# Retention outputs from a packed state, one join on another engine, and a reordered middle step

## The chip, the cores and the metric

The kernel runs on 1 core of one Trainium2 chip. The metric is the device time of one launch in microseconds. The kernel before has three timed runs: 305.37, 305.54 and 307.35 us, median 305.54 us.

## The reference, cut to what matters

```python
def _attn_ref(q, k, v):                      # q, k, v: (8, 8, 576, 64)
    scores = scale * np.matmul(q, k.transpose(0, 1, 3, 2))
    gamma = 1.0 - 2.0 ** (-5.0 - np.arange(H))
    rel = pos[:, None] - pos[None, :]
    Dmat = np.where(rel >= 0, gamma[:, None, None] ** rel, 0.0)
    return np.matmul(scores * Dmat, v)

def _moe_ref(x, w_in, w_out):                # (4608,512) (512,2048) (2048,512)
    h = x @ w_in
    g = h * np.clip(h + 3.0, 0.0, 6.0) / 6.0
    return g @ w_out

x = attn_out.transpose(0, 2, 1, 3).reshape(4608, 512)
out = _moe_ref(x, w_in, w_out)
```

So there is a retention (attention without softmax, with a decay for each head) over 8 batches, 8 heads, 576 positions and 64 columns a head, and behind it a feed-forward layer of two matrix products over the 4608 tokens.

## The kernel before, in words

**Pieces.** Each batch is cut into four pieces of 128 positions ("main", numbered i = 0 to 3 within the batch) and a rest of 64; the rests of two batches make one piece ("rest"). For each piece the output is the sum of an inner part (masked scores times v) and a part from the state of the pieces before it. The eight heads go as four pairs; a pair fills the 128 partitions, 64 for each head.

**The state.** `update_mm` (L362) makes each piece's own contribution k'v for all heads by 64-column matmuls into a PSUM tile `u`, in the bank with the tag `tu`, of which there is one. `update_state` (L379) has VectorE add the state before it (L390) and scale by the decay (L391); the result `ts` is packed: 128 partitions x 4 pairs x 64, with head 2p in partitions 0 to 63 and head 2p+1 in 64 to 127. ScalarE then copies its two halves (L403, L404) into a tile `tbd` of 128 x 4 x 128, in which the two heads of a pair stand on the diagonal and the rest is zero. `inter` (L325) multiplies `tbd` with the queries: one 128x128 matmul for each pair (L339). A piece with i = 0 has no state before it and `inter` issues nothing for it; so of four main pieces three have these matmuls. The first batch is made apart, by `state_early`, which writes block-diagonal tiles directly.

**Scores.** `scores` (L307) makes scores in 64-row matmuls, the two heads of a pair into two PSUM banks, and VectorE masks them (L318). `scores_second` (L656) does the same for a second piece in two banks of the tag `ph`. `intra` (L345) adds the inner part into the same bank as `inter`, and ScalarE copies the bank to `xt`, the input of the feed-forward (L356).

**Feed-forward.** It goes in blocks of 512 tokens. `gemm1` makes 16 units for each block: four matmuls into a `ph` bank (L417), a ScalarE and a VectorE instruction on it (L424, L425). For blocks 2 to 7 the second product is one Strassen-Winograd step with seven half-size products (`product`, L511) that accumulate in three banks `b`, `a` and `c`, and `gather` (L529) reads partial sums out: products 1, 6 and 7 from `b` and 5 from `c` by ScalarE copies (L535), the joins for the quarters of the output by VectorE (L538, L543), by GpSimd (L541, the quarter C22 from two SBUF copies) and by ScalarE (L546).

**Order.** The order on each engine is the order of the program text. `seven_block` (L708) mixes the products of one block with the pieces of the block after the next: up to one rest (`alone`) and the four main pieces c0 to c3, two at a time. Its middle step, between products 6 and 5, is: `inter` of c0 and c1, the second in a bank of the tag `ph`; scores and `update_mm` of c2 and c3; `intra` of c0 and c1. Its last step, between products 3 and 4, is `inter` and `intra` of c2 and c3. Five blocks (2 to 6) have four main pieces; block 7 has a rest alone. Block 1 uses `step` (L679), which does the same between units of an ordinary second product. The second batch (pieces 4 to 7) is made in `first_step` (L621), between units of block 0; there the `inter` matmuls are at L641. The tag `ph` has four banks, `o`, `tu` one each and `sc` two banks.

Of the kernel before, what the change touches and what calls it, by code (L numbers as in the profile page):

```python
# [11 lines left out]
FP16 = mybir.dt.float16  # L12
# [5 lines left out]
def kernel(  # L18
# [20 lines left out]
    P = 128  # L39
# [129 lines left out]
        nc.scalar.copy(gqv[:, 0], gq[:, :, None].to_broadcast([P, H, D]))  # L169

    tbd = []
    for i in range(5):
        t = const.tile([P, NPAIR, P], FP16, name=f"tbd{i}")
        if i >= EARLY:
            nc.vector.memset(t, 0.0)
        tbd.append(t)

    warmed = [0]

# [19 lines left out]

    st = {}  # L200
    later = []
    free_tbd = list(range(5))
    state_of = {}

    def run_later(n):
        for _ in range(n):
# [54 lines left out]
    def out_last(c):  # L261
        before, qk = st[c]["before"], st[c]["qk"]
        at, vs = st[c]["at"], st[c]["vs"]
        kb, g0 = place_of(c)
        halves = [psum.tile([P, NPAIR, P], FP32, tag="o", name=f"o_{c}"),
                  psum.tile([P, NPAIR, P], FP32, tag="ph", bufs=4, name=f"o2_{c}")]
        for i, o in enumerate(halves):
            for p in range(2):
                nc.tensor.matmul(o[:, p, :], tbd[before][:, 2 * i + p, :], qk[:, 0, 2 * i + p, :],
                                 start=(p == 0), stop=False, skip_group_check=True)  # L270
        for i, o in enumerate(halves):
            for p in range(2):
                for h2 in range(2):
                    r = slice(h2 * HALF, h2 * HALF + HALF)
                    nc.tensor.matmul(o[r, p, :], vs[:, 4 * i + 2 * p + h2, :],
                                     at[:, h2, 2 * i + p, :],
                                     start=False, stop=(p == 1), skip_group_check=True)
            nc.scalar.copy(xt_of(kb)[:, 2 * i:2 * i + 2, g0:g0 + P], o[:, 0:2, :])  # L278

    def state_early(c):  # L280

        kn, vs = loaded[c]["kn"], st[c]["vs"]
        u = psum.tile([P, NPAIR, P], FP32, tag="tu", name=f"u_{c}")
        old = st[c]["before"] = state_of.get(0)
        for p in range(NPAIR):
            nc.tensor.matmul(u[:, p, :], kn[:, 2 * p:2 * p + 2, :], vs[:, 2 * p:2 * p + 2, :],
                             start=(p == 0), stop=(old is None and p == NPAIR - 1),
                             skip_group_check=True)
        if old is not None:
            nc.tensor.matmul(u, ident16, tbd[old], start=False, stop=True,  # L290
                             skip_group_check=True)
            free_tbd.append(old)
        new = free_tbd.pop(0)
        state_of[0] = new
        later.append(lambda: nc.vector.tensor_tensor(out=tbd[new], in0=u, in1=gfull,
                                                     op=ALU.mult))

    def transpose_k(c):
# [26 lines left out]
    def inter(c, tag="o"):  # L325
        kind, b, i, _ = pieces[c]
        o = psum.tile([P, NPAIR, P], FP32, tag=tag, bufs=4 if tag == "ph" else 1, name=f"o_{c}")
        st[c]["o"] = o
        st[c]["first"] = True
        if kind == "main" and i == 0:  # L330
            return
        qk = st[c]["qk"]
        if kind == "main":
            states = [(st[c].get("before", state_of[b]), slice(0, P))]
        else:
            states = [(state_of[2 * b], slice(0, HALF)), (state_of[2 * b + 1], slice(HALF, P))]
        for j, (state, cols) in enumerate(states):
            for p in range(NPAIR):
                nc.tensor.matmul(o[:, p, cols], tbd[state][:, p, :], qk[:, 0, p, cols],  # L339
                                 start=(j == 0 and p == 0), stop=False, skip_group_check=True)  # L340
            if kind == "rest" or st[c].get("last_reader"):
                free_tbd.append(state)
        st[c]["first"] = False

    def intra(c, copy_later=False, more=False):  # L345
# [33 lines left out]
    def update_state(c, copies_later=False):  # L379
# [5 lines left out]
        ts = work.tile([P, NPAIR, D], FP16, tag="ts", bufs=2, name=f"ts_{c}")  # L385
        if i == 0:
            nc.vector.tensor_tensor(out=ts, in0=u, in1=scale, op=ALU.mult)  # L387
        else:
            ta = work.tile([P, NPAIR, D], FP32, tag="ta", bufs=2, name=f"ta_{c}")
            nc.vector.tensor_tensor(out=ta, in0=u, in1=st[c - 1]["ts"], op=ALU.add)  # L390
            nc.vector.tensor_tensor(out=ts, in0=ta, in1=scale, op=ALU.mult)  # L391
        st[c]["ts"] = ts
        old = state_of.get(b)
        new = free_tbd.pop(0)
        state_of[b] = new
        if old is not None and st[c].get("o") is not None:
            free_tbd.append(old)
        elif old is not None:
            st[c]["before"] = old
            st[c]["last_reader"] = True  # L400

        def copies():
            nc.scalar.copy(tbd[new][0:HALF, :, 0:D], ts[0:HALF])  # L403
            nc.scalar.copy(tbd[new][HALF:P, :, D:2 * D], ts[HALF:P])  # L404

        if copies_later == "given":
            return copies
        if copies_later:
            later.append(copies)
        else:  # L410
            copies()

    gts = {}

# [114 lines left out]
    def gather(kb, which):  # L529

        my = seven[kb]
        if which in (1, 6, 7, 5):
            my[which] = work.tile([P, 2, half_n], FP32, tag=f"part{which}", bufs=1,
                                  name=f"part{which}_{kb}")
            nc.scalar.copy(my[which], my["c" if which == 5 else "b"])  # L535
# [2 lines left out]
            nc.vector.tensor_tensor(out=my["lo"][:, :, lo_n], in0=my[1], in1=my["a"], op=ALU.add)  # L538
        if which == 7:
            my["hi"] = work.tile([P, 2, DM], FP32, tag="osb2", bufs=3, name=f"ohi_{kb}")  # L540
            nc.gpsimd.tensor_tensor(out=my["hi"][:, :, hi_n], in0=my[7], in1=my[5], op=ALU.add)  # L541
# [79 lines left out]
    def first_step(c):  # L621
# [3 lines left out]
        if old:  # L625
# [6 lines left out]
            update_state(c - 1, copies_later=True)  # L632
        if new:
            q_by_pe(c + 1)
        if old and new:
# [72 lines left out]
    def seven_block(kb, mine, next_):  # L708
# [4 lines left out]
        copies = {}  # L713

        def both(which):
            for tt in range(2):
                product(kb, which, tt)

        def state(c):
            copies[c] = update_state(c, copies_later="given")  # L720

        def begin(one, other):
            masks[one] = scores(one, given=True)
            masks[other] = scores_second(other, given=True)
            update_mm([one, other])

        def end(*cs):
            for c, tag in zip(cs, ("o", "ph")):
                inter(c, tag)

        def done(*cs):
            for c in cs:
                st.pop(c - 3, None)
                loaded.pop(c)

        masks = {}
# [6 lines left out]
        if c0 is not None and not alone:  # L743
            begin(c0, c1)
        both(1)
        gather(kb, 1)
        if alone:
            end(*alone)
            if c0 is not None:
                begin(c0, c1)  # L750
            intra(alone[0])
        if c0 is not None:
            masks[c0]()
            state(c0)
            copies[c0]()
            masks[c1]()
            load_until(c1 + NBUF)
        elif alone:
            load_until(alone[0] + NBUF)
        done(*alone)  # L760
        both(2)
        gather(kb, 2)
        if c0 is not None:
            state(c1)
        both(6)
        gather(kb, 6)
        if c0 is not None:
            end(c0, c1)
            begin(c2, c3)
            intra(c0)  # L770
            intra(c1)
            copies[c1]()
        sum_of(kb, 3, 0, 8)
        if c0 is not None:
            masks[c2]()
        sum_of(kb, 4, 0, 8)
        if c0 is not None:
            state(c2)
            done(c0, c1)
            load_until(c3 + NBUF)  # L780
        both(5)
        gather(kb, 5)
        if c0 is not None:
            masks[c3]()
        both(7)
        gather(kb, 7)
        if c0 is not None:
            copies[c2]()
            state(c3)
        both(3)  # L790
        if c0 is not None:
            end(c2, c3)
            intra(c2)
            intra(c3)
            done(c2, c3)
# [1 line left out]
            ahead(c)  # L797
        gather(kb, 3)
        both(4)
        if c0 is not None:  # L800
            copies[c3]()
        gather(kb, 4)
        for c in next_[2:]:
            ahead(c)
# [89 lines left out]
```

## Time and profile before

| | |
|---|---|
| median of the runs | 305.54 us |
| the profiled execution's own time | 305.33 us |
| its span, first to last instruction | 303.6 us |
| granted TensorE clock, mean | 0.994 |
| TensorE busy in the stretch 90 to 240 us | 28.8 to 29.1 us of every 30 |
| VectorE busy in the same stretch | 26.9 to 27.9 us of every 30 |
| ScalarE busy in the same stretch | 18.0 to 19.0 us of every 30 |
| `tbd` copies on ScalarE, L403 and L404 | 28 each, 11.3 and 11.2 us together |

The profiled execution took 1.7 us more than its span, for what lies before the first and behind the last instruction. In the rows of the profile a matmul stands as PE with the number of rows and columns of the array that it uses (128*128, 64*128, 128*64) and then the shape that goes through; PEld is the load of the weights. A duration of one matmul, such as 219 ns, runs from issue to the end in the array; matmuls are pipelined, so what a run of matmuls costs is read from the starts of successive rows.

### The profile page before, as it was taken

The numbers are of one execution on the slowest core, as the hardware profiler recorded it, in microseconds if no ns is written. First come the engines' busy times: TensorE is split into PE (matmuls) and PEld (weight loads), VectorE is DVE, ScalarE is ACT, GpSimd is POOL, SyncE is SP. The second block draws the span as 40 slices with busy tenths as digits, with TensorE's granted clock in tenths as the row PEclk, the third lists the DMA queues.
The fourth block names the chain that finished last, engine by engine and source line by source line (L and its number), as shares of the span: only waits on it lengthen the run. The fifth ranks groups of instructions, "written<-read, shape, count | busy, mean of one in ns | idle before, by whom it ended". The sixth has DMA issues, their size and how long they took to land.

```text
span 303.6 us, 6408 instructions
## 1 busy us (share of the span) xinstructions
PE 287.9 (95%) x2526; PEld 177.9 (59%) x2526; DVE 228.6 (75%) x372; ACT 178.0 (59%) x307; POOL 117.7 (39%) x141
## 2 busy tenths in 40 slices
PE   5989998999999989998999899989999899999995
PEld 2644445544544777467745784578448754884444
DVE  4748666797749998899889997999799849727700
ACT  5558436784558546855676557745773587327611
POOL 8983577736612295076500980485000100010000
PEclk9799999999999999999999999999999999999999
DMA  9999999999999499999992999799730030012022
GB/s 71 146 192 207 189 159 216 168 129 155 155 175 96 102 133 106 231 81 125 91 244 54 96 125 217 85 128 85 201 76 2 17 141 2 0 56 86 1 69 71
DMA packets 152976, 35.56 MB, mean 117 GB/s; under 512 B 143601, under 2 KB 148465, under 8 KB 152945
## 3 DMA queue, kind: packets, MB, share of 16 engines
q0 software_dynamic: 117264, 18.36, 85.0%
q1 hardware_dynamic: 35280, 16.26, 26.1%
q10 hardware_dynamic: 400, 0.52, 0.5%
q8 instruction: 20, 0.33, 0.4%
q14 instruction: 12, 0.09, 0.1%
HBM read 36.70 MB, written 9.44 MB: 152 GB/s over the span
## 4 chain that ended last, share of the span: by engine, by line
PE 76%; DMA 8%; DVE 5%; ACT 4%; POOL 4%; issue 1%; POOLq 0%; DVEq 0%; ACTq 0%
PE ph L417 35%; PE b L525 12%; PE pout L474 8%; PE c L525 7%; DMA wout<-in_moe_w_out_dram 5%; PE a L525 4%; DMA win<-in_moe_w_in_dram 3%; PE o L350 3%; POOL qv L102 2%; ACT xt L356 2%; DVE at L318 2%; PE u L374 2%; PE sc L314 1%; PE o L339 1%; POOL kn L102 1%; PE pout L559 1%
## 5 line engine op out<-in xcount | busy, mean ns | idle before, releaser
L425 DVE SCALAR_TENSOR_TENSOR gt<-u,ph 128x512 f16<-128x512 f32 x144 | 97.4, 686 | 31.6 <-ACT u L424 29.4
L424 ACT ACTIVATE u<-ph,cb 128x512 f32<-128x512 f32 x144 | 98.3, 687 | 25.7 <-PE ph L417 24.5
L417 PE MATMUL ph<-xt,win 128*128 128x512 f16 x496 | 108.4, 379 | 0.6 <-ACT xt L278 0.4
L417 PEld LDWEIGHTS <-win 128*128 128x128 f16 x560 | 54.8, 98 | 65.1 <-issue 0.7
L102 POOL DMA_DIRECT2D kn<-in_k_dram x40 | 34.6, 869 | 78.0 <-PE u L374 39.8
L525 PEld LDWEIGHTS <-s 128*128 128x128 f16 x384 | 37.5, 98 | 9.3 <-issue 4.6
L474 PE MATMUL pout<-wout,gt 128*128 128x512 f16 x176 | 39.6, 379 | 0.0
L102 POOL DMA_DIRECT2D qv<-in_v_dram x40 | 34.7, 874 | 4.2 <-DMA wout<-in_moe_w_out_dram 1.7
L102 POOL DMA_DIRECT2D qv<-in_q_dram x40 | 34.5, 866 | 4.8 <-DMA wout<-in_moe_w_out_dram 3.2
L541 POOL TENSOR_TENSOR ohi<-part,part 128x512 f32<-128x512 f32 x6 | 8.8, 1462 | 62.2 <-ACT part L535 60.7
L525 PEld LDWEIGHTS <-gt 128*128 128x128 f16 x288 | 26.9, 98 | 4.3
L474 PEld LDWEIGHTS <-gt 128*128 128x128 f16 x176 | 16.8, 98 | 19.1
L318 DVE TENSOR_TENSOR at<-sc,mask_wide 128x1024 f16<-128x1024 f32 x19 | 23.2, 1219 | 5.1 <-PE sc L314 5.0
L535 ACT COPY part<-b 128x512 f32<-128x512 f32 x18 | 10.6, 586 | 27.2 <-PE b L525 27.2
L356 ACT CAST xt<-o 128x512 f16<-128x512 f32 x31 | 17.0, 589 | 13.5 <-PE o L350 11.2
L304 DVE TENSOR_TENSOR vs<-qv,gqv 128x1024 f16<-128x1024 f16 x28 | 23.4, 874 | 0.6 <-DMA qv<-in_v_dram 0.6
L525 PE MATMUL b<-tw,s 128*128 128x256 f16 x192 | 22.9, 273 | 0.0
L507 DVE TENSOR_TENSOR s<-gt 128x512 f16<-128x512 f16 (+1 forms) x30 | 17.4, 578 | 0.1
L403 ACT COPY tbd<-ts 64x256 f16<-64x256 f16 x28 | 11.3, 404 | 9.0 <-DVE ts L387 5.6
L478 ACT COPY osb<-pout 128x512 f32<-128x512 f32 x11 | 6.5, 587 | 17.0 <-PE pout L474 16.9
L525 PE MATMUL c<-tw,s 128*128 128x256 f16 x96 | 11.4, 272 | 4.7 <-ACT xt L356 4.7
L672 DVE TENSOR_TENSOR at<-sc,mask_wide 128x512 f16<-128x512 f32 x24 | 15.4, 681 | 0.0
(91 smaller groups left out, 280.1 us busy)
## 6 DMA issues: line engine op xcount, KB each, us to landing
kn<-in_k_dram POOLq DMA_DIRECT2D x32, 128.0 KB, 4.5
qv<-in_q_dram POOLq DMA_DIRECT2D x32, 128.0 KB, 5.2
qv<-in_v_dram POOLq DMA_DIRECT2D x32, 128.0 KB, 5.6
out_dram<-olo SPq DMA_DIRECT2D x6, 512.0 KB, 3.6
out_dram<-ohi SPq DMA_DIRECT2D x6, 512.0 KB, 4.3
wout<-in_moe_w_out_dram POOLq DMA_DIRECT2D x4, 512.0 KB, 14.6
out_dram<-osb SPq DMA_DIRECT2D x8, 256.0 KB, 5.5
win<-in_moe_w_in_dram POOLq DMA_DIRECT2D x3, 512.0 KB, 10.6
```

Of the source, the lines that this page charges most:

```text
L102: nc.gpsimd.dma_start(dst[p0:p0 + n], src[b, :, s0:s0 + n, :].rearrange("h s d -> s h d"))
L304: nc.vector.tensor_tensor(out=vs, in0=loaded[c]["qv"], in1=gqv, op=ALU.mult)
L318: mask = lambda: nc.vector.tensor_tensor(out=at.rearrange("t a b s -> t (a b) s"), in0=sc.rearrange("t a b s -> t (a b) s"), in1=mask_b[pi ...
L356: nc.scalar.copy(xt_of(kb)[:, :, g0:g0 + P], o)
L403: nc.scalar.copy(tbd[new][0:HALF, :, 0:D], ts[0:HALF])
L417: nc.tensor.matmul(ph, win16[:, dmc, P * fc:P * fc + P], xt_of(kb)[:, dmc, :], start=(dmc == 0), stop=(dmc == NCC - 1))
L424: nc.scalar.activation(u, ph, ACTF.Relu, bias=cb[:, 0:1], scale=1.0 / 6.0)
L425: nc.vector.scalar_tensor_tensor(out=gts[kb][:, fc, :], in0=u, scalar=1.0, in1=ph, op0=ALU.min, op1=ALU.mult)
L474: nc.tensor.matmul(pout, gt[:, fc, P * mc:P * mc + P], wout16[:, fc, :], start=(fc == 0), stop=(fc == NFC - 1))
L507: nc.vector.tensor_tensor(out=sm[i][:, q], in0=one, in1=other, op=op)
L525: nc.tensor.matmul(my[chain][:, tt], left[:, k, P * tt:P * tt + P], right[:, k, :], start=(first and tt == 0 and k == 0), stop=(k == half_ ...
L672: nc.vector.tensor_tensor(out=at[:, h2], in0=banks[h2], in1=mask[:, None, :].to_broadcast([P, NPAIR, P]), op=ALU.mult)
```

## The change

There are three parts. (1) `ts` itself is the state: `state_mm` multiplies it by 64x64 matmuls, two for each pair of heads, one in rows and columns 0 to 63 of the array and one in 64 to 127, both into the same PSUM bank. The `tbd` copies go, and `tbd` stays for the first batch only. The tile `ts` has four buffers, and three more (`tf`) for the state behind a batch's last piece. (2) C22 is joined by VectorE, from the SBUF copy of product 5 and directly from the bank `b`; the ScalarE copy of product 7 and the GpSimd add go. (3) In the middle step c1's output is in the bank `tu`, `inter` and `intra` of c0 and c1 come ahead of the scores of c2 and c3, and `update_mm` of c2 and c3 is between the two halves of product 5. `update_state` of c1 is ahead of the VectorE join of product 2.

```diff
+    def state_mm(o, state, qk, cols, start, stop):
+        for p in range(NPAIR):
+            if state.shape[-1] == P:
+                nc.tensor.matmul(o[:, p, cols], state[:, p, :], qk[:, 0, p, cols],
...
+                continue
+            for h2 in range(2):
+                r = slice(h2 * HALF, h2 * HALF + HALF)
+                nc.tensor.matmul(o[r, p, cols], state[r, p, :], qk[r, 0, p, cols],
...
@@ inter
-            for p in range(NPAIR):
-                nc.tensor.matmul(o[:, p, cols], tbd[state][:, p, :], qk[:, 0, p, cols],
-                                 start=(j == 0 and p == 0), stop=False, skip_group_check=True)
-            if kind == "rest" or st[c].get("last_reader"):
-                free_tbd.append(state)
+            state_mm(o, state, qk, cols, j == 0, False)
@@ update_state
-        def copies():
-            nc.scalar.copy(tbd[new][0:HALF, :, 0:D], ts[0:HALF])
-            nc.scalar.copy(tbd[new][HALF:P, :, D:2 * D], ts[HALF:P])
...
+            st[c]["before"] = state_of[b]
+        state_of[b] = ts
@@ gather
-        if which in (1, 6, 7, 5):
+        if which in (1, 6, 5):
...
-            nc.gpsimd.tensor_tensor(out=my["hi"][:, :, hi_n], in0=my[7], in1=my[5], op=ALU.add)
+            nc.vector.tensor_tensor(out=my["hi"][:, :, hi_n], in0=my[5], in1=my["b"], op=ALU.add)
@@ first_step
-            for p in range(NPAIR):
-                nc.tensor.matmul(o[:, p, :], tbd[before][:, p, :], st[c - 1]["qk"][:, 0, p, :],
-                                 start=False, stop=(p == NPAIR - 1), skip_group_check=True)
+            state_mm(o, before, st[c - 1]["qk"], slice(0, P), False, True)
@@ seven_block
         both(2)
+        if more:
+            update_state(c1)
         gather(kb, 2)
-        if c0 is not None:
-            state(c1)
         both(6)
         gather(kb, 6)
-        if c0 is not None:
-            end(c0, c1)
-            begin(c2, c3)
+        if more:
+            end(c0, c1, "tu")
             intra(c0)
             intra(c1)
-            copies[c1]()
+            score(c2, c3)
         sum_of(kb, 3, 0, 8)
-        if c0 is not None:
+        if more:
             masks[c2]()
         sum_of(kb, 4, 0, 8)
-        if c0 is not None:
-            state(c2)
+        product(kb, 5, 0)
+        if more:
+            update_mm([c2, c3])
+            update_state(c2)
             done(c0, c1)
             load_until(c3 + NBUF)
-        both(5)
+        product(kb, 5, 1)
         gather(kb, 5)
...
         both(7)
         gather(kb, 7)
-        if c0 is not None:
-            copies[c2]()
-            state(c3)
+        if more:
+            update_state(c3)
         both(3)
-        if c0 is not None:
-            end(c2, c3)
+        if more:
+            end(c2, c3, "ph")
             intra(c2)
             intra(c3)
```

Here `end(one, other, tag)` calls `inter` for both, the second with that bank; `score` is `begin` without `update_mm`.

More of the change, by code (lines that the diff above doesn't have):

```diff
@@ L171 @@
     tbd = []
[L172 to L176, printed above, removed]
+    for i in range(EARLY):
+        tbd.append(const.tile([P, NPAIR, P], FP16, name=f"tbd{i}"))
     warmed = [0]
@@ L201 @@
     later = []
-    free_tbd = list(range(5))
     state_of = {}
+    def state_mm(o, state, qk, cols, start, stop):
+        for p in range(NPAIR):
+            if state.shape[-1] == P:
+                nc.tensor.matmul(o[:, p, cols], state[:, p, :], qk[:, 0, p, cols],
+                                 start=(start and p == 0), stop=(stop and p == NPAIR - 1),
+                                 skip_group_check=True)
+                continue
+            for h2 in range(2):
+                r = slice(h2 * HALF, h2 * HALF + HALF)
+                nc.tensor.matmul(o[r, p, cols], state[r, p, :], qk[r, 0, p, cols],
+                                 start=(start and p == 0), stop=(stop and p == NPAIR - 1),
+                                 skip_group_check=True)
     def run_later(n):
@@ L268, in out_last @@
             for p in range(2):
-                nc.tensor.matmul(o[:, p, :], tbd[before][:, 2 * i + p, :], qk[:, 0, 2 * i + p, :],
+                nc.tensor.matmul(o[:, p, :], before[:, 2 * i + p, :], qk[:, 0, 2 * i + p, :],
                                  start=(p == 0), stop=False, skip_group_check=True)
@@ L289, in state_early @@
         if old is not None:
-            nc.tensor.matmul(u, ident16, tbd[old], start=False, stop=True,
+            nc.tensor.matmul(u, ident16, old, start=False, stop=True,
                              skip_group_check=True)
[L292 to L295, printed above, removed]
+        new = state_of[0] = tbd[c]
+        later.append(lambda: nc.vector.tensor_tensor(out=new, in0=u, in1=gfull,
                                                      op=ALU.mult))
@@ L377, in update_mm, with update_state @@
                                      skip_group_check=True)
-    def update_state(c, copies_later=False):
+    def update_state(c):
         kind, b, i, _ = pieces[c]
@@ L384, in update_state @@
         scale = gc_b[1 if i == PER - 1 and b % 2 else 0]
-        ts = work.tile([P, NPAIR, D], FP16, tag="ts", bufs=2, name=f"ts_{c}")
+        tag, bufs = ("tf", 3) if i == PER - 1 else ("ts", 4)
+        ts = work.tile([P, NPAIR, D], FP16, tag=tag, bufs=bufs, name=f"ts_{c}")
         if i == 0:
@@ L389, in update_state @@
             ta = work.tile([P, NPAIR, D], FP32, tag="ta", bufs=2, name=f"ta_{c}")
-            nc.vector.tensor_tensor(out=ta, in0=u, in1=st[c - 1]["ts"], op=ALU.add)
+            nc.vector.tensor_tensor(out=ta, in0=u, in1=state_of[b], op=ALU.add)
             nc.vector.tensor_tensor(out=ts, in0=ta, in1=scale, op=ALU.mult)
[L392 to L400, printed above, removed]
-        def copies():
[L403 to L411, printed above, removed]
+            st[c]["before"] = state_of[b]
+        state_of[b] = ts
     gts = {}
@@ L631, in first_step @@
             load_until(c - 1 + NBUF)
-            update_state(c - 1, copies_later=True)
+            update_state(c - 1)
         if new:
@@ L712, in seven_block @@
         alone, (c0, c1, c2, c3) = mine[:single], mine[single:] or [None] * 4
-        copies = {}
+        more = c0 is not None
+        masks = {}
         def both(which):
@@ L717, in both, with score, end @@
                 product(kb, which, tt)
-        def state(c):
-            copies[c] = update_state(c, copies_later="given")
-        def begin(one, other):
+        def score(one, other):
             masks[one] = scores(one, given=True)
             masks[other] = scores_second(other, given=True)
[L725 to L729, printed above, removed]
+        def end(one, other, tag):
+            inter(one)
+            inter(other, tag)
         def done(*cs):
@@ L734, in done @@
                 loaded.pop(c)
-        masks = {}
         run_later(9)
@@ L742, in seven_block @@
         sum_of(kb, 2, 4, 8)
-        if c0 is not None and not alone:
-            begin(c0, c1)
+        if more and not alone:
+            score(c0, c1)
+            update_mm([c0, c1])
         both(1)
@@ L747, in seven_block @@
         if alone:
-            end(*alone)
-            if c0 is not None:
-                begin(c0, c1)
+            inter(alone[0])
+            if more:
+                score(c0, c1)
+                update_mm([c0, c1])
             intra(alone[0])
-        if c0 is not None:
+        if more:
             masks[c0]()
-            state(c0)
-            copies[c0]()
+            update_state(c0)
             masks[c1]()
@@ L761, in seven_block @@
         both(2)
+        if more:
+            update_state(c1)
         gather(kb, 2)
-        if c0 is not None:
-            state(c1)
         both(6)
         gather(kb, 6)
-        if c0 is not None:
-            end(c0, c1)
-            begin(c2, c3)
+        if more:
+            end(c0, c1, "tu")
             intra(c0)
             intra(c1)
-            copies[c1]()
+            score(c2, c3)
         sum_of(kb, 3, 0, 8)
-        if c0 is not None:
+        if more:
             masks[c2]()
         sum_of(kb, 4, 0, 8)
-        if c0 is not None:
-            state(c2)
+        product(kb, 5, 0)
+        if more:
+            update_mm([c2, c3])
+            update_state(c2)
             done(c0, c1)
             load_until(c3 + NBUF)
-        both(5)
+        product(kb, 5, 1)
         gather(kb, 5)
-        if c0 is not None:
+        if more:
             masks[c3]()
@@ L786, in seven_block @@
         gather(kb, 7)
-        if c0 is not None:
-            copies[c2]()
-            state(c3)
+        if more:
+            update_state(c3)
         both(3)
-        if c0 is not None:
-            end(c2, c3)
+        if more:
+            end(c2, c3, "ph")
             intra(c2)
@@ L799, in seven_block @@
         both(4)
-        if c0 is not None:
-            copies[c3]()
         gather(kb, 4)
```

## The prediction

> **What bounds the kernel now.** I read the page first, for the engines and the chain of waits, then the list of waits, and then the timeline of the places where a wait stands in it.
>
> ```profile
> PE 287.9 (95%) x2526; PEld 177.9 (59%) x2526; DVE 228.6 (75%) x372; ACT 178.0 (59%) x307; POOL 117.7 (39%) x141
> ...
> PE 76%; DMA 8%; DVE 5%; ACT 4%; POOL 4%; issue 1%; POOLq 0%; DVEq 0%; ACTq 0%
> ```
>
> TensorE is busy for 95% of the span and carries 76% of the chain that ended last. DVE, at 75% over the whole, is the next candidate, since the change gives it work. From the page alone, then, only two things can shorten the run: fewer microseconds of TensorE work, or fewer of its waits. The list of waits has one large entry with TensorE as the waiting engine:
>
> ```profile
> PE c L525 <- ACT xt L356: 4.7, 5, 0.9
> ```
>
> Five times, once in each of the five blocks with four main pieces, product 5 finds no bank for `c` until ScalarE has copied the output of c1 out of a `ph` bank: 0.9 us each. This is the middle step that the change reorders. Its timeline in one block (start, length, engine, line, operation; rows of PE, ACT and DVE):
>
> ```profile
> 136.63 1.28 DVE L672 TENSOR_TENSOR at<-sc,mask_wide 128x512 f16<-128x512 f32 x2
> ...
> 137.83 0.68 DVE L538 TENSOR_TENSOR olo<-part,a 128x512 f32<-128x512 f32 x1
> ...
> 138.42 0.41 DVE L390 TENSOR_TENSOR ta<-u,ts 128x256 f32<-128x256 f32 x1
> ...
> 138.72 0.39 PE L339 MATMUL o<-qk,tbd 128*128 128x128 f16 x4
> 138.87 0.42 DVE L391 TENSOR_TENSOR ts<-ta,gc 128x256 f16<-128x256 f32 x1
> 138.92 0.59 ACT L535 COPY part<-b 128x512 f32<-128x512 f32 x1 [1.36 <-PE b L525]
> ...
> 139.04 0.40 PE L314 MATMUL sc<-qk 64*128 64x128 f16 x8
> 139.21 1.22 DVE L507 TENSOR_TENSOR s<-gt 128x2048 f16<-128x2048 f16 x1
> ...
> 139.28 0.39 PE L664 MATMUL sc<-qk 64*128 64x128 f16 x8
> ...
> 139.59 0.44 PE L374 MATMUL u<-vs,kn 128*64 128x64 f16 x16
> ...
> 139.87 0.62 PE L350 MATMUL o<-at,vs 128*64 128x128 f16 x16
> ...
> 140.30 1.07 ACT L356 CAST xt<-o 128x512 f16<-128x512 f32 x2 [0.79 <-PE o L350]
> 140.35 1.22 DVE L318 TENSOR_TENSOR at<-sc,mask_wide 128x1024 f16<-128x1024 f32 x1
> ...
> 141.43 1.91 PE L525 MATMUL c<-tw,s 128*128 128x256 f16 x16 [0.94 <-ACT xt L356]
> ...
> 141.48 1.21 DVE L507 TENSOR_TENSOR s<-gt,s 128x2048 f16<-128x2048 f16 x1
> ...
> 143.17 1.91 PE L525 MATMUL b<-tw,s 128*128 128x256 f16 x16
> ...
> 143.48 1.28 DVE L672 TENSOR_TENSOR at<-sc,mask_wide 128x512 f16<-128x512 f32 x2
> 144.68 0.41 DVE L390 TENSOR_TENSOR ta<-u,ts 128x256 f32<-128x256 f32 x1
> ...
> 146.66 0.61 PE L339 MATMUL o<-qk,tbd 128*128 128x128 f16 x8
> ...
> 147.20 0.64 PE L350 MATMUL o<-at,vs 128*64 128x128 f16 x16
> ...
> 147.77 1.92 PE L525 MATMUL b<-tw,gt 128*128 128x256 f16 x16
> ```
>
> The lengths include the way through the array, so a cost is the distance to the next start. Four matmuls of L339 and the change to the next form take 139.04 - 138.72 = 0.32 us, eight 147.20 - 146.66 = 0.54; so four take 0.22 (55 ns each) and **a change of the array's form about 0.10**. Eight score matmuls with no change behind them take 0.24, with one (139.28 to 139.59) 0.31, so about 0.22 by themselves: half of L339's time for each, since a row half runs beside the other. Sixteen of `u` take 0.28, sixteen of L350 0.57 less a change, 0.47. A product takes 1.74 (141.43 to 143.17), half of one 0.87.
>
> **Part 1, the middle step.** From the end of product 6 to the start of product 7 it now takes 143.17 - 138.72 = 4.45 us. Behind the change the same stretch holds, with a change of form ahead of each item: c1's state matmuls, eight of 64x64; sixteen of `intra`; sixteen scores; half of product 5; `u`; the other half. That is six changes, 0.60, and 0.22 + 0.47 + 0.45 + 0.87 + 0.28 + 0.87 = 3.16: together 3.76, if nothing waits and the eight take the 0.22 of eight scores. The gain is 0.69, taken as **0.7, five times: 3.5 us**. The 0.94 of the wait goes and two and a half changes of form come.
>
> What could be late next, with T = 138.72 as the step's start. (a) c1's output now takes the bank `tu`, so it needs VectorE's read of `u`. That read (L390) is now ahead of L538: from about 137.85 to 138.3, 0.4 before T. (b) Product 5's bank is now the one that L538 frees; L538 runs behind L390 and L391 and ends at about 139.4, and TensorE comes to it at T + 0.10 + 0.22 + 0.10 + 0.47 + 0.10 + 0.45 + 0.10 = 140.3, with 0.9 to spare. (c) `u` of c2 and c3 needs c1's bank copied out. The first copy starts 0.43 behind the first matmul of `intra` now (139.87 to 140.30), so it would at 139.57, behind the copy of 138.92 that ends at 139.51; the two take 1.07 and end at 140.65. TensorE comes to `u` at 140.3 + 0.87 + 0.10 = 141.2: 0.55 to spare. Behind `u`, whose start moves from 139.59 to 141.2, stand the loads that `load_until` puts on GpSimd's queue; they fill buffers for the block after the next stage, and this queue idles before them now, so 1.6 us later costs nothing. (d) VectorE's own row: from 137.85 it has L390, L391, L538, L507, L318, L507, L390, L391, two of L672 and then the new join; by the distances above (0.45, 0.35, 0.6, 1.14, 1.13, 1.13, 0.5, 0.35, 1.2) these reach 144.7, and product 7 ends at 138.72 + 3.76 + 1.74 = 144.2. So the join doesn't hold the queue for TensorE, and ends at about 145.4.
>
> **Part 2, the join.** Product 4 writes `b` again and now waits for that join. TensorE comes to it at 144.2 + 1.74 + 1.2 = 147.1, 1.7 us behind. For VectorE the join costs some 0.6 to 0.68 us (L538 has the same form), for GpSimd and ScalarE it takes away what follows:
>
> ```profile
> L541 POOL TENSOR_TENSOR ohi<-part,part 128x512 f32<-128x512 f32 x6 | 8.8, 1462 | 62.2 <-ACT part L535 60.7 <-DVE ts L391 1.5
> ...
> L339 PE MATMUL o<-qk,tbd 128*128 128x128 f16 (+1 forms) x112 | 8.4, 212 | 0.0
> ```
>
> Neither was on TensorE's path: I cost it at zero. If the 1.7 us of cover were gone, it would be 0.7 a block, 4 us.
>
> **Part 3, the other state products.** L339 stands 112 times: 18 products of four matmuls in blocks 1 to 6, four rests of eight, and two products of the first batch, which stay as they are. At the last step of each of five blocks eight become sixteen in half the time each, with one change of form more: 0.10 lost, 0.5 in all. Block 1 has two such places: 0.2 lost. The rests stand ahead of a score that waits for a mask anyway, 0.2 us in each such block: zero.
>
> No trace of before has a 64x64 matmul. Below, it can't be under the 27 ns of the score matmuls' pace, as the same 128 columns stream through; above, if the two of a pair don't run side by side, it is the 55 ns of L339 for each, 0.22 more for a product. I take the lower end: column halves into one bank (L350, 16 in 0.47) and row halves into two banks (L664, 8 in 0.22) both run at 27 to 29 ns, and the new form differs from both at once. The Trainium skill, TensorEngine Tiling (Array Packing), section Restrictions and Gotchas, speaks against this: it says that different row tiles can't access the same PSUM bank simultaneously, and here the two of a pair do write one bank, though other partitions of it. No row of this trace has that case; by that page each product would cost the upper end. It is the first rival below.
>
> **Part 4, the second batch.** Here the copies that go are on the path:
>
> ```profile
> 46.08 0.40 PE L226 MATMUL trk<-ident,kn 128*128 128x128 f16 x4
> ...
> 46.31 1.89 PE L474 MATMUL pout<-wout,gt 128*128 128x512 f16 x8
> 46.34 0.40 ACT L403 COPY tbd<-ts 64x256 f16<-64x256 f16 x1
> 46.76 0.40 ACT L404 COPY tbd<-ts 64x256 f16<-64x256 f16 x1
> ...
> 47.18 0.59 ACT L227 COPY qk<-trk 128x512 f16<-128x512 f16 x1
> 47.33 0.42 DVE L213 TENSOR_TENSOR vs<-qv,gqv 128x512 f16<-128x512 f16 x1
> 47.66 0.59 ACT L356 CAST xt<-o 128x512 f16<-128x512 f32 x1
> ...
> 48.31 0.41 PE L350 MATMUL o<-at,vs 128*64 128x128 f16 x8
> ...
> 49.80 0.40 ACT L403 COPY tbd<-ts 64x256 f16<-64x256 f16 x1
> ...
> 50.64 0.59 ACT L227 COPY qk<-trk 128x512 f16<-128x512 f16 x1
> 50.82 0.41 DVE L213 TENSOR_TENSOR vs<-qv,gqv 128x512 f16<-128x512 f16 x1
> 51.12 0.59 ACT L356 CAST xt<-o 128x512 f16<-128x512 f32 x1
> 51.77 0.41 PE L350 MATMUL o<-at,vs 128*64 128x128 f16 x8 [0.95 <-ACT xt L356]
> ```
>
> At 48.31 and 51.77 TensorE starts as the copy to `xt`, which frees the bank `o`, has ended; ahead of it on ScalarE stand two copies to `tbd`, 0.84 us. Without them, at the first place the `xt` copy ends by 47.7, and the eight matmuls of L474 (0.215 each, two of them filling 0.43) end at 48.04; with a change of form TensorE goes on at 48.14, 0.17 earlier. At the second place the next to end is VectorE's `vs`: 51.23, less those 0.17, so a start at 51.1 instead of 51.77: 0.65 in all. The state matmuls of these steps cost one change of form more each, of which one lies on the path: **0.55 gained**, between 0.2 and 0.8.
>
> **The sum.** 3.5 - 0.5 - 0.2 + 0.55 = 3.35, say 3.4 us. From about 58 us on TensorE is the path nearly without a break, so a microsecond saved there stays saved. The profiled execution took 305.33 us (its span of 303.6 and 1.7 around it), and the median of the runs is 0.2 above it: 301.9 for an execution like the profiled one, **302.1 us** for the median.
>
> **The rivals.** *The two 64x64 matmuls of a pair wait for each other, as they write one bank.* 21 products on the path (18, and three in the second batch) then cost 0.22 more: 4.6 us, and the time is 306.7, a little slower than before. The point from which it decides is 3.4 / 21 = 0.16 us a product, that is, 48 ns for each of the eight in place of 27. If each wait were also a drain such as a change of form shows (0.10), eight would take 1.2 us, and 21 products 21 us more: about 323. For it speaks that in the trace the two row halves of the scores are always in two banks; against it, that the partitions differ and column halves share a bank at full pace. I give 0.12 to the first price and 0.06 to the second.
>
> *The wait moves.* Product 5, or `u` behind it, waits for VectorE or ScalarE as it now does for the `xt` copy; the margins of 0.9 and 0.55 are short against queues with instructions of 1.2 us. If half of the 0.7 goes so in each block, the time is 302.1 + 1.75 = 303.9. Chance 0.10.
>
> *VectorE becomes the bound.* In a stretch of 30 us (columns: PE, PEld, DVE, ACT, POOL busy) it has 27.8 us of work:
>
> ```profile
> 120.00:150.00 30.00, 29.06 (x282) 19.91 (x281) 27.79 (x44) 18.75 (x33) 14.76 (x16) 1.00 1.26 131
> ```
>
> It gets 0.65 more for each block, while TensorE's period falls by 0.6. 28.5 in 30 still fits, and 1.7 us of cover stand ahead of product 4; were it used up, 4 us would be lost: 306. Chance 0.03.
>
> **How the numbers follow.** The forecast has the remaining 0.69; its own range, from the bounds of part 4 and 0.1 us either way for each middle step, is 301.3 to 302.8. The range that I give goes on to the moved wait, 301.2 to 304.0, which leaves out the cases of the shared bank and the full VectorE, about 0.2. This kernel's measurement tells about 1%, 3.06 us, from no change: faster by that means under 302.5, which most of the forecast's own range is but not all. That makes 0.58 for faster, 0.36 for the same (the top of the forecast's range, the moved wait, serial pairs, VectorE) and 0.06 for slower.
>
> **What would show it.** In the profile of the changed kernel: the starts of a pair's two matmuls some 3 to 4 ns or 55 ns apart, and eight of them in 0.22 or 0.45 us; no entry of product 5 waiting for L356's copy, and none in its place for `u`; the distance from product 6's end to product 7's start about 3.75 us; 1.2 us from product 3's end to product 4; the second batch's waits on the `xt` copy gone. The prediction is wrong if the pair's starts are a whole matmul apart, or if the middle stretch stays over 4.2 us.

## The result, and the profile after

The changed kernel takes 302.91 us (median of nine runs, 302.19 to 304.75); the kernel before took 305.97 us in its nine runs beside it (305.37 to 308.88). The ratio is 0.989, with a 95% interval of 0.985 to 0.993: 1.1% faster, and 302.1 was forecast. In a second comparison, the first experiment below, the same kernel took 303.3 us, with a ratio of 0.993 (0.991 to 0.996).

The profiled execution of the changed kernel took 304.75 us with a span of 303.0, only 0.6 below the span of before. One must not compare these two spans as they stand. The page first (engines, then shares of the chain that ended last):

```profile
PE 291.4 (96%) x2638; PEld 176.4 (58%) x2638; DVE 227.0 (75%) x377; ACT 152.4 (50%) x245; POOL 109.0 (36%) x135
...
PE 88%; POOL 4%; DVE 3%; DMA 2%; ACT 1%; issue 1%; POOLq 0%
```

ScalarE lost 26 us of work and GpSimd 9. TensorE's share of the chain rose from 76% to 88% here, but in another execution of the same kernel (the first experiment) it is 79%, since there the beginning of the chain runs through loads (DMA 9% in place of 2%); so this share says little of the change. The chain of waits, in order of time, gives the two marks that I use from here on: the start of block 1's stretch of 48 matmuls, and the last copy (start, length, what). Of the kernel before:

```profile
58.54 10.52 PE ph L417 x48
...
299.88 0.37 ACT osb L563
```

Of the changed kernel:

```profile
60.39 10.52 PE ph L404 x48
...
299.27 0.37 ACT osb L550
```

Between the marks lie 241.34 us before and 238.88 after: **2.46 us less**. Ahead of the first mark this execution is 1.85 us late. The start varies from execution to execution, and what is seen in this one is the following. The stretch 18 to 24 us, by engine (columns: length, busy time of PE, PEld, DVE, ACT, POOL with counts, granted clock, DMA share, GB/s), before:

```profile
18.00:24.00 6.00, 5.65 (x36) 2.69 (x34) 2.91 (x5) 3.90 (x7) 4.21 (x6) 1.00 1.24 204
```

and after:

```profile
18.00:24.00 6.00, 5.05 (x29) 2.52 (x29) 0.26 (x1) 1.62 (x4) 5.54 (x7) 0.72 1.24 204
```

The timeline of GpSimd and TensorE just there, before:

```profile
16.15 1.15 POOL L213 TENSOR_TENSOR vs<-qv,gqv 128x512 f16<-128x512 f16 x1 [0.42 <-DMA qv<-in_v_dram]
...
17.36 0.38 PE L286 MATMUL u<-vs,kn 128*128 128x128 f16 x4 [0.41 <-POOL vs L213]
```

and in the changed kernel:

```profile
17.49 1.15 POOL L223 TENSOR_TENSOR vs<-qv,gqv 128x512 f16<-128x512 f16 x1 [1.77 <-DMA qv<-in_v_dram]
...
18.69 0.40 PE L296 MATMUL u<-vs,kn 128*128 128x128 f16 x4 [1.83 <-POOL vs L223]
```

In the changed kernel's profile GpSimd waited 1.77 us for the load of piece 3's v (0.42 before), its scaling came late, TensorE stood 1.83 us (0.41 before), and the granted clock of the stretch was 0.72. By piece 4's inner part (45.05 before, 47.47 after) it is 2.4 us behind. Up to there both programs issue the same loads and the same matmuls, and among the seven kernels below, whose code is the same up to there but for what is said of the last, that inner part starts anywhere from 45.0 to 47.1 us. So the two marks, and the distance from piece 4's inner part to the first mark, tell more of a change of 1% than one execution's span does.

The middle step in the same block as before (from the start of the three products ahead of it to the start of the state matmuls it is 5.34 us here and 5.25 before; the 0.09 more is the change of form, so product 6 ends 0.09 ahead of L211's start, at 140.27):

```profile
139.36 0.41 DVE L395 TENSOR_TENSOR ta<-u,ts 128x256 f32<-128x256 f32 x1
...
140.15 0.68 DVE L525 TENSOR_TENSOR olo<-part,a 128x512 f32<-128x512 f32 x1
...
140.36 0.41 PE L211 MATMUL o<-qk,ts 64*64 64x128 f16 x8
...
140.70 0.64 PE L354 MATMUL o<-at,vs 128*64 128x128 f16 x16
...
141.15 1.07 ACT L360 CAST xt<-o 128x512 f16<-128x512 f32 x2
...
141.27 0.40 PE L322 MATMUL sc<-qk 64*128 64x128 f16 x8
...
141.50 0.39 PE L649 MATMUL sc<-qk 64*128 64x128 f16 x8
...
141.82 1.05 PE L512 MATMUL c<-tw,s 128*128 128x256 f16 x8
...
142.80 0.44 PE L378 MATMUL u<-vs,kn 128*64 128x64 f16 x16
...
143.17 1.05 PE L512 MATMUL c<-tw,s 128*128 128x256 f16 x8
...
144.05 1.91 PE L512 MATMUL b<-tw,s 128*128 128x256 f16 x16
...
146.15 0.68 DVE L528 TENSOR_TENSOR ohi<-part,b 128x512 f32<-128x512 f32 x1
...
147.64 0.63 PE L211 MATMUL o<-qk,ts 64*64 64x128 f16 x16
...
148.21 0.64 PE L354 MATMUL o<-at,vs 128*64 128x128 f16 x16
...
148.78 1.92 PE L512 MATMUL b<-tw,gt 128*128 128x256 f16 x16
```

No row of PE has a wait in brackets any more. From product 6's end to product 7's start it is 144.05 - 140.27 = 3.78 us (4.45 before), in all five blocks alike. The eight 64x64 matmuls take 140.70 - 140.36 = 0.34 with one change of form, so 0.24: the pace of the scores. The two of a pair start 3 to 4 ns apart, and pairs follow every 52 to 56 ns, but for the first behind a change. The margins held: the read of `u` that frees c1's bank (L395) ends 0.5 us ahead of the step, L525, which frees product 5's bank, ends 1.0 us before product 5 starts, `u` starts 0.58 us after the `xt` copies have ended (142.22), and product 4 nearly 2 us after the join.

The second batch, where the copies to `tbd` stood ahead of the copy to `xt`:

```profile
48.73 1.89 PE L461 MATMUL pout<-wout,gt 128*128 128x512 f16 x8
...
49.42 0.59 ACT L360 CAST xt<-o 128x512 f16<-128x512 f32 x1
...
50.55 0.41 PE L354 MATMUL o<-at,vs 128*64 128x128 f16 x8
...
52.84 0.59 ACT L360 CAST xt<-o 128x512 f16<-128x512 f32 x1
...
53.07 0.41 DVE L223 TENSOR_TENSOR vs<-qv,gqv 128x512 f16<-128x512 f16 x1
...
53.54 0.41 PE L354 MATMUL o<-at,vs 128*64 128x128 f16 x8 [0.36 <-DVE vs L223]
```

The `xt` copy is now out of the way at both places: at 50.55 TensorE goes on as the matmuls of L461 end, at 53.54 it waits for VectorE's `vs`. From piece 4's inner part to block 1's stretch it is 60.39 - 47.47 = 12.92 us, 13.49 before: **0.57 us less**. With the 2.46 that makes 3.03. The medians differ by 3.06, but in the second comparison by 2.44 (305.74 and 303.3), so agreement to 0.03 is in part luck.

### The profile page after: what moved, and what is told of

Its sections match the earlier page's. It is cut to its first block, busy times and chain, and to the rows that moved or that the text cites. A ratio compares the mean times of both kernels' runs of the same rounds, so it can differ in the third digit from the quotient of the medians.

```text
span 303.0 us, 6540 instructions
## 1 busy us (share of the span) xinstructions
PE 291.4 (96%) x2638; PEld 176.4 (58%) x2638; DVE 227.0 (75%) x377; ACT 152.4 (50%) x245; POOL 109.0 (36%) x135
## 4 chain that ended last, share of the span: by engine, by line
PE 88%; POOL 4%; DVE 3%; DMA 2%; ACT 1%; issue 1%; POOLq 0%
PE ph L404 40%; PE pout L461 12%; PE b L512 12%; PE c L512 7%; PE a L512 4%; PE o L354 3%; DMA qv<-in_v_dram 2%; PE o L211 2%; POOL qv L102 2%; PE sc L322 2%; PE u L378 2%; DVE at L326 2%; POOL kn L102 1%; PE pout L546 1%; ACT u L411 1%; DVE gt L412 1%
## 5 line engine op out<-in xcount | busy, mean ns | idle before, releaser
L461 PE MATMUL pout<-wout,gt 128*128 128x512 f16 x176 | 39.7, 379 | 0.0
L512 PEld LDWEIGHTS <-s 128*128 128x128 f16 x384 | 36.7, 98 | 4.9
L461 PEld LDWEIGHTS <-gt 128*128 128x128 f16 x176 | 16.7, 98 | 19.1
L522 ACT COPY part<-b 128x512 f32<-128x512 f32 x12 | 7.0, 587 | 28.0 <-PE b L512 28.0
L312 DVE TENSOR_TENSOR vs<-qv,gqv 128x1024 f16<-128x1024 f16 x28 | 18.1, 685 | 1.0 <-DMA qv<-in_v_dram 1.0
L404 PE MATMUL ph<-xt_rest,win 128*128 128x512 f16 x64 | 14.0, 379 | 0.0
L354 PE MATMUL o<-at,vs 128*64 128x128 f16 x280 | 12.1, 222 | 0.4 <-DVE vs L223 0.4
L512 PE MATMUL c<-tw,s 128*128 128x256 f16 x96 | 12.4, 274 | 0.0
```

Source lines behind the costliest of these rows:

```text
L312: nc.vector.tensor_tensor(out=vs, in0=loaded[c]["qv"], in1=gqv, op=ALU.mult)
L354: nc.tensor.matmul(o[r, p, :], vs[:, 2 * p + h2, :], at[:, h2, p, :], start=(st[c]["first"] and p == 0), stop=(p == NPAIR - 1 and not more ...
L404: nc.tensor.matmul(ph, win16[:, dmc, P * fc:P * fc + P], xt_of(kb)[:, dmc, :], start=(dmc == 0), stop=(dmc == NCC - 1))
L461: nc.tensor.matmul(pout, gt[:, fc, P * mc:P * mc + P], wout16[:, fc, :], start=(fc == 0), stop=(fc == NFC - 1))
L512: nc.tensor.matmul(my[chain][:, tt], left[:, k, P * tt:P * tt + P], right[:, k, :], start=(first and tt == 0 and k == 0), stop=(k == half_ ...
```

## The experiments

**The changed kernel again.** No edit.

> The changed kernel again, nothing altered. In its first profile block 1's stretch of 48 matmuls starts at 60.39 us, against 58.54 before, and from there to the last copy it takes 238.9 us against 241.3. If the late start is a late landing of piece 3's v and the slower clock behind it, as I think, it comes and goes: in an execution without it the stretch starts at 57.8 to 58.2, the 238.9 stay within 0.1, and the time is 302.2 to 302.9. If the change itself brought the late start (rival), the stretch starts at 60 us again.

Measured: 303.3 us; the first mark at 59.26, the last copy at 298.14, so 238.88 again. The start was neither early nor as late as in the first profile: piece 4's inner part came at 46.34 and the stretch began 12.92 later. The part behind the mark repeats to 0.01 us, what lies ahead of it doesn't. The time that I gave was for an early start, which did not come, so this run doesn't test it; nor does one start between the two settle the rival. The four kernels after this one, which have the same code up to the mark, do: their stretch begins at 60.02, 58.63, 58.43 and 58.26 us. The late start comes and goes with the same code, so it is not the change's.

**The bank alone undone.**

```diff
-            end(c0, c1, "tu")
+            end(c0, c1, "ph")
```

> The changed kernel with c1's output back in a bank of the tag ph; the new order stays. If the bank is what took the wait away, product 5 finds no bank again until both outputs are copied: from the rows of the changed kernel the copies end at 142.22 and product 5 starts at 141.82, so some 0.45 us come back in each of five blocks; the stretch from product 6's end to product 7 takes 4.2 instead of 3.78, the part behind 58 us 241.1 instead of 238.9, the time is 2.2 us above the changed kernel's. If the order alone took it away (rival), nothing changes: 3.78 and 238.9.

Measured: 305.64 us, ratio 0.999 (0.997 to 1.002) to the kernel before. The list of waits has product 5's entry again, at less than half its size (total, times, longest),

```profile
PE c L512 <- ACT xt L360: 2.0, 5, 0.4
```

and the timeline of TensorE shows where:

```profile
141.58 0.39 PE L649 MATMUL sc<-qk 64*128 64x128 f16 x8
142.36 1.03 PE L512 MATMUL c<-tw,s 128*128 128x256 f16 x8 [0.39 <-ACT xt L360]
```

The middle stretch is 4.24, the part between the marks 60.02 to 301.13, 241.11 us: 2.23 more than with the bank `tu`. The rival falls: without the other bank product 5 waits again, 0.39 us a block where it was 0.94 before the change. So the new order, with the later `update_mm`, takes a part of the wait away, and the bank takes away the rest.

**The order alone undone.**

```diff
-            intra(c0)
-            intra(c1)
             score(c2, c3)
+            intra(c0)
+            intra(c1)
```

> The changed kernel with the middle step's scores ahead of the inner parts of c0 and c1, as before; the bank tu and the place of update_mm stay. The copies to xt then start 0.55 us later and end about when TensorE comes to u. If the bank does nearly all, u waits 0 to 0.2 us a block and the time grows by 0 to 0.8 us. If the order is what matters (rival), u waits as product 5 did before, 0.5 to 0.9 a block, and the time grows by 2.5 us or more.

Measured: 303.76 us; the middle stretch 3.83, between the marks 58.63 to 297.69, 239.06. With the bank `tu` in place the order is worth 0.04 us a block, 0.2 in all: the small end of what I expected. It keeps `u` from touching the end of the copies, no more.

**The whole middle step as before, with the packed state.**

```diff
-            end(c0, c1, "tu")
-            intra(c0)
-            intra(c1)
-            score(c2, c3)
+            end(c0, c1, "ph")
+            score(c2, c3)
+            update_mm([c2, c3])
+            intra(c0)
+            intra(c1)
...
-            update_mm([c2, c3])
             update_state(c2)
```

> The changed kernel with the whole middle step as before: c1's output in ph, scores and update_mm of c2 and c3 ahead of the inner parts; the packed state and VectorE's join stay. By my sum the packed state costs one change of form more at each of its places (0.10 us) and gains only in the second batch (0.55): product 5 waits 0.9 again, the middle stretch takes 4.45 + 0.10 = 4.55, the part behind 58 us 242.6 against 241.3 before, and the time is 0.6 to 0.7 above the kernel before. If the packed state itself, by the ScalarE copies that it drops, is where the gain is from (rival), the time stays 1 us or more below the kernel before.

Measured: 306.66 us, ratio 1.0045 (1.003 to 1.006): slower than the kernel before. Product 5's wait is back whole:

```profile
PE c L512 <- ACT xt L360: 4.7, 5, 0.9
```

The middle stretch is 4.56, between the marks lie 58.43 to 301.18, 242.75 us, 1.41 more than before; the time is 0.9 above the kernel before, where 0.6 to 0.7 was expected. From piece 4's inner part to the first mark it is 12.91 us here, 12.92 in the changed kernel. So the packed state costs time in every block and gives 0.57 in the second batch; all the rest of the gain is the middle step's. Against this kernel the changed one gains 3.87 between the marks, more than the 2.2 of the bank and the 0.2 of the order together: with the bank `ph`, the new order and the later `update_mm` are worth 242.75 - 241.11 = 1.64. The place of `update_mm` was not undone alone.

**The join back on GpSimd.**

```diff
-        if which in (1, 6, 5):
+        if which in (1, 6, 7, 5):
...
-            nc.vector.tensor_tensor(out=my["hi"][:, :, hi_n], in0=my[5], in1=my["b"], op=ALU.add)
+            nc.gpsimd.tensor_tensor(out=my["hi"][:, :, hi_n], in0=my[7], in1=my[5], op=ALU.add)
```

> The changed kernel with C22 joined by GpSimd from two SBUF copies again, and product 7 copied by ScalarE; all else stays. I costed this part at zero, since no matmul waits for it: the part behind 58 us takes 238.9 within 0.2. VectorE has 0.65 us less in each block, but its v and q scalings beside GpSimd's add take 1.2 to 1.5 us instead of 0.65. If VectorE's load sets the pace (rival), the kernel gets faster here by up to 0.65 a block, 3 us in all; if GpSimd's add was in the way (the other rival), it gets slower by as much as its beside-running scalings lost, 1.6 us a block.

Measured: 303.09 us; between the marks 58.26 to 297.15, 238.89. The join costs and gives nothing on the path, whichever engine does it. On VectorE the scalings of v and q (columns: busy us, mean ns, idle before) are, with the join on GpSimd,

```profile
L312 DVE TENSOR_TENSOR vs<-qv,gqv 128x1024 f16<-128x1024 f16 x28 | 23.0, 856 | 1.0 <-DMA qv<-in_v_dram 1.0
```

and in the changed kernel

```profile
L312 DVE TENSOR_TENSOR vs<-qv,gqv 128x1024 f16<-128x1024 f16 x28 | 18.1, 685 | 1.0 <-DMA qv<-in_v_dram 1.0
```

so VectorE gets 4.1 us of joins (six of 684 ns) and is rid of 4.9 us of slower scalings.

**The copies back in the second batch, into a tile without a reader.**

```diff
+    spare = const.tile([P, NPAIR, P], FP16, name="spare")
...
+    def spare_copies(ts):
+        nc.scalar.copy(spare[0:HALF, :, 0:D], ts[0:HALF])
+        nc.scalar.copy(spare[HALF:P, :, D:2 * D], ts[HALF:P])
...
             update_state(c - 1)
+            ts = state_of[b]
+            later.append(lambda: spare_copies(ts))
```

> The changed kernel with the two half copies of the state put back on ScalarE in the second batch alone, into a tile that nobody reads. It prices the gain there. From intra of piece 4 to block 1's stretch of matmuls the kernel before took 13.49 us (45.05 to 58.54) and the changed one 12.92 (47.47 to 60.39). If the copies on ScalarE are the cause, the distance is 13.4 to 13.6 again and the time 0.55 us above the changed kernel's; if the shorter distance came from something else (rival), it stays at 12.9.

Measured: 303.6 us. The chain:

```profile
45.59 0.41 PE o L354 x8
...
59.23 10.52 PE ph L404 x48
```

That is 13.64 us, 0.72 more than without the copies and a little above what I expected; between the marks it stays at 238.89. TensorE's wait for the copy to `xt`, which the kernel before has and the changed one hasn't, is back (total, times, longest):

```profile
PE o L354 <- ACT xt L360: 0.9, 1, 0.9
```

So the copies cost 0.72. The kernel before, with copies, took 13.49, 0.15 less than this one; the changes of form of the state matmuls would account for it, but that was not measured apart. The whole time, 303.6, lies 0.7 and 0.3 above the two medians of the changed kernel, which themselves differ by 0.4, so the 0.55 can't be read from it.

**Block-diagonal tiles again, in the new order.** The second batch and the rests stay packed; from the third batch on c0, c1 and c2 go through `bd` tiles and 128x128 matmuls.

```diff
+    def diagonal(b):
+        ts, t = state_of[b], bd[made[0] % 4]
+        made[0] += 1
+        state_of[b] = t
+        def copies():
+            nc.scalar.copy(t[0:HALF, :, 0:D], ts[0:HALF])
+            nc.scalar.copy(t[HALF:P, :, D:2 * D], ts[HALF:P])
+        return copies
...
             update_state(c0)
+            diagonal(pieces[c0][1])()
...
             intra(c1)
+            copies[c1]()
             score(c2, c3)
...
         gather(kb, 5)
         if more:
+            copies[c2]()
             masks[c3]()
```

The four tiles are set to zero by VectorE during block 0, and `update_state` adds to the packed state.

> The new middle step and join, but from the third batch on the state goes through block-diagonal tiles again (copied by ScalarE for c0, c1 and c2, which have a reader among the main pieces) and 128x128 matmuls; the second batch and the rests stay packed. By my sum the 64x64 form saves no TensorE time and costs a change of form at each place. Without it the middle stretch takes 3.68 instead of 3.78, product 3's end to product 4's start 1.11 instead of 1.23, block 1 saves 0.2: the part behind 58 us takes 237.7 instead of 238.9, and the time is 1.2 us below the changed kernel's, about 301.6. If ScalarE's six copies a block are in the way of the xt copies (rival), u or product 4 waits for them and the time is that of the changed kernel or above.

Measured: **300.84 us** (300.59 to 301.33), ratio 0.985 (0.982 to 0.987) to the kernel before. The middle step and the last step of the same block:

```profile
137.28 0.39 PE L222 MATMUL o<-qk,bd 128*128 128x128 f16 x4
137.60 0.64 PE L371 MATMUL o<-at,vs 128*64 128x128 f16 x16
...
140.96 1.91 PE L529 MATMUL b<-tw,s 128*128 128x256 f16 x16
...
144.45 0.61 PE L222 MATMUL o<-qk,bd 128*128 128x128 f16 x8
144.99 0.64 PE L371 MATMUL o<-at,vs 128*64 128x128 f16 x16
145.56 1.92 PE L529 MATMUL b<-tw,gt 128*128 128x256 f16 x16
```

From product 6 to 7 it is 3.68 us, from product 3 to 4 1.11. Between the marks lie 57.88 to 295.35, 237.47, that is 1.41 less than in the changed kernel, where 1.2 was expected. ScalarE's copies lie beside other work: no wait of TensorE for them, or for a later `xt` copy, comes back in this stretch. The time is 0.8 below the 301.6 expected and 2.1 to 2.5 below the changed kernel's two medians; Of that, 1.41 lies between the marks and the rest outside them, where the beginning differs by as much from execution to execution. This version beats both kernels.

## Why the prediction was right, point by point

- **Product 5's wait** was the term that decided, and it went as said: 3.78 us against the 3.76 of the sum. The gain is 0.67 a block, 3.3 us in five; I had rounded it up to 0.7 and 3.5. Undone alone, the bank brings 2.2 us back and the order 0.2; with bank, order and the place of `update_mm` undone together 3.87 us come back (242.75 - 238.88). So the parts overlap and can't be added: without the bank the other two still take 1.64.
- **What could be late next** was late nowhere: the margins for c1's bank, product 5, `u` and the join were 0.5, 1.0, 0.58 and about 2 us where I had 0.4, 0.9, 0.55 and 1.7.
- **The 64x64 matmuls** run in pairs at the lower end of the price. The first rival, that a pair waits because it writes one bank, fell: 3 to 4 ns apart. The rule that I had set against it, from the Trainium skill, TensorEngine Tiling (Array Packing), section Restrictions and Gotchas, does not hold for two row tiles that write different partitions of a bank. Two row tiles on the same partitions of a bank were not tried.
- **The changes of form** were sized a little low: the last step takes 1.23 (148.78 - 147.64 = 1.14, and 0.09 for the change ahead of L211) instead of 1.11, 0.12 a block and not 0.10, 0.6 us in all. Block 1 lost 0.23 (17.67 to 17.90 us from its first scores to the next stretch), 0.2 said. The rests cost nothing, as said: from the start of product 1 to the scores behind a rest it is 2.37 us in both kernels. So the part behind the mark gained 3.3 - 0.6 - 0.2 = 2.5, measured 2.46; the sum had 2.8.
- **The second batch** gained 0.57, 0.55 said, and for the reason given: the copy out of the way, then VectorE's `vs` next.
- **The join** at zero: 0.01 us, by the kernel that puts it back. VectorE's load didn't set the pace, then.
- **The two other rivals** fell with the traces: no new wait of TensorE in the middle step, and VectorE did not become the bound, since taking the join from it gained nothing.

The sum was 3.4 us and the measured parts give 3.03: the mechanism was right, and the sizes of the middle step and of the last step's change of form were a little too good. The measured 302.91 is 0.8 above the 302.1 of the forecast. It lies at the top end of the forecast's own range (I wrote 302.8; the two bounds added give 302.95), and well inside the wider one only by the room that I had left for a moved wait, which didn't come. About 0.4 of the 0.8 is the sum; another 0.4 is that the kernel before took 305.97 us beside it, not 305.54. The forecast's margin over 1% was thin, and the two comparisons, 1.1% and 0.7%, lie on either side of it. In the profiled executions the part behind the mark repeats to 0.01 us, while with the same code the mark itself lies anywhere from 58.3 to 60.4 us. So the beginning is the likely cause, but the executions behind the medians have no trace that would show it.

## What to carry to other kernels

A wait for a bank is priced by who holds the bank and when it comes free: here the new order and the later `update_mm` removed more than half of product 5's wait (0.94 to 0.39 us), and another bank for the output the rest. Once the bank was there, the order was worth only 0.2 us in all, so undo such parts alone and together before giving one of them the gain. In this kernel four zero-padded 128x128 matmuls cost about as much as their eight 64x64 halves side by side (0.22 and 0.24 us), so packing the operand gained TensorE nothing, and lost a change of form wherever its neighbours were 128x128; it paid only where the padding copies stood on the path. Copies are worth removing where something waits behind them, so ask that of each place apart: here they were on the path in one batch of eight, and the best version keeps them elsewhere.

## What the runs showed of the hardware that I had not expected

The GpSimd add beside VectorE's 16-bit scalings made these slower by a quarter in the mean over all 28 (856 ns against 685), but not evenly: with the join on GpSimd 23 of them take 0.68 to 0.69 us as they do without it, and five take 1.16 to 2.46. Three of the five overlap an add in the trace, and the other two end some 0.3 us before one starts; the spans on GpSimd are rough. Taking the add away paid VectorE for the join. The Trainium skill, SBUF — State Buffer, section SBUF: two separate sides, says that these two engines share a port pair which one of them holds for a whole instruction; a few long scalings among unchanged ones agree with this, though the two that overlap no add are not explained.

And in the changed kernel's first profile a single late load in the first 18 us stood ahead of more than its own lateness: TensorE stood 1.4 us longer than before, the granted clock of the next stretch was 0.72, and by 45 us the kernel was 2.4 us behind. That the stand brought the lower clock is not shown: the kernel before has 0.72 too, in its stretch from 6 to 12 us.
